# Channel-mix products on tiles of one batch in four pairs, in one fixed order with the attention before them

## The chip, the cores and the metric

The kernel runs on one NeuronCore of a Trainium2 chip. The metric is device time in microseconds of one execution. One execution was also recorded by the hardware profiler; times inside the kernel come from that record. TensorE is called PE, VectorE DVE, ScalarE ACT, and SyncE, which issues every DMA here, SP.

## What is computed

Attention with a sigmoid in place of the softmax, and behind it a channel mix on its output x (8 batches of 448 tokens, 768 features):

```python
scores = q @ k.T / sqrt(64) - log(448)          # 8 batches, 12 heads, 448 tokens, 64 features
x = sigmoid(scores) @ v                         # -> [8, 448, 768]
x_prev = x shifted by one token in each batch
xk = mu_k * x + (1 - mu_k) * x_prev
xr = mu_r * x + (1 - mu_r) * x_prev
k = maximum(xk @ w_k, 0)                        # 768 -> 1024
v = (k * k) @ w_v                               # 1024 -> 768
r = sigmoid(xr @ w_r)                           # 768 -> 768
out = r * v
```

The weights come as 64-bit floats and are converted on the chip; activations are 32-bit. 8 x 448 = 3584 tokens.

## The kernel before

**Attention** goes over 48 pairs of heads, `n` from 0 to 47, six pairs to a batch (`b, j = divmod(n, 6)`), two pairs to a pass of its loop. For each pair PE computes three score chunks of 128 keys (L341) into three score buffers `sc`, ACT turns each into `pf` by the sigmoid (L362), and PE multiplies `pf` with `v` into `av` (L369); the last 64 keys go in a tail (`score_tails` L350, `pt`, `weigh_tails` L377). `gather` copies `av` to `xx` (ACT, L387), makes the difference to the token before (`dx`, L388) and the two mixes `mr` and `mk` (L391) on DVE, and writes them to DRAM as `xr_d[j]` and `xk_d[j]`, columns of batch `b`. Beside this the conversion of `w_r` runs (`convert_seven`), with its results in seven buffers `slot`, and a first part of `w_k`.

**The products** come in three stages: R (`xr @ w_r`), K (`xk @ w_k`), V (`k*k @ w_v`). The weights are cut into four quarters, and two token tiles at a time are combined so that seven products do the work of eight (`ORDER`, products named `p` = 0 to 6 with weights in `slot` number `POS[p]`). One product of one pair of tiles is a *step*: for every row block `i` (3, 4, 3 in R, K, V) and contraction tile `t` (3, 3, 4) three matmuls (`multiply`, L556), high weight x high operand, high x low, low x high, since each 32-bit value is split into two parts. That is 27, 36 and 36 matmuls in a step of R, K and V. `right` makes a step's operands: `fetch` loads a tile into `ys`, `minus` (DVE, L464) forms sums of tiles, `operand` casts it on ACT (L472) and subtracts on DVE to get the low part (L473) into one of ten buffers `rr`. Four of the `ys` and `rr` are set aside from the start (`PRE`), the others (`ysb`, `rrb` in the trace) lie in memory that attention uses and can be filled only when attention is over. `evacuate` reads the sums from PSUM (`xb`, `yb`) on ACT and DVE; four matmuls (`prime`, L543) open the `yb` sums once.

A token tile is 512 tokens here, so a tile takes in parts of two batches. 3584 tokens are seven tiles: three pairs and a single one, for which four of the seven products suffice (`ODD`), two of which use the operands of the other two again. That is 3 x 7 + 4 = 25 steps in a stage.

**Order of the work.** `Plan` collects every operation with its engine, an estimated duration, a due time (`at`, in steps) and what it reads and writes. A list scheduler in `order` runs through it with estimated times and picks on each free engine the ready operation that is due first; `emit` issues them in that order. There are two plans, one for attention with the `w_r` conversion and one for the products, and each is issued inside a `tc.manual_schedule()` of its own, which keeps the order as issued. Between the two, outside of both, buffers are closed and opened. The framework below joins both lists, and an operation of the second whose buffers are free can come to stand among those of the first.

Of the kernel before, what the change touches and what calls it, by code (L numbers as in the profile page):

```python
# [8 lines left out]
F32 = mybir.dt.float32  # L9
# [13 lines left out]
class Plan:  # L23
# [8 lines left out]
    def op(self, engine, cost, prio, run, reads, writes, dma=None):  # L32
        i = len(self.ops)
        deps = set()
        for r in reads:
            if r in self.writer:
                deps.add(self.writer[r])
        for w in writes:
            if w in self.writer:
                deps.add(self.writer[w])  # L40
            deps.update(self.readers.get(w, ()))
        for r in reads:
            self.readers.setdefault(r, []).append(i)
        for w in writes:
            self.writer[w] = i
            self.readers[w] = []
        deps.discard(i)
        self.ops.append(Op(engine, cost, prio, run, deps, dma))
# [50 lines left out]
def attention_then_channel_mix(  # L99
# [16 lines left out]
    P = 128  # L116
    N, _, S = q.shape
# [2 lines left out]
    D = v.shape[-1]  # L120
    NP = DM // P
    B = N // NP
    T = 512
    NT = B * S // T
    NJ, NF = DM // P, DF // P
    NC = S // P
    KW = NC * P
# [5 lines left out]
    R_, K_, V_ = range(3)  # L133
# [10 lines left out]
    mur = const.tile([P, NJ], F32, name="mur")  # L144
    muk = const.tile([P, NJ], F32, name="muk")

    def scratch(name, n):
        return [dram.tile([P, B * S], F32, name=f"{name}{i}") for i in range(n)]

    xk_d, xr_d, r_d, k2_d = scratch("xk_d", NJ), scratch("xr_d", NJ), scratch("r_d", NJ), scratch("k2_d", NF)  # L150
# [10 lines left out]
    def ring(pool, name, bufs, shape, dtype):  # L161
        return [pool.tile(shape, dtype, name=f"{name}{i}") for i in range(bufs)]

    def gap(pool, name, size):
        pool.tile([P, size // 4], F32, name=name)
# [9 lines left out]
    gap(base, "gap0", 64)  # L175
    rr = ring(base, "rr", PRE, [P, 2, T], F32R)
    ys = ring(base, "ys", PRE, [P, T], F32)
    wraw = ring(base, "wraw", 2, [P, WP, 2], U32)
# [17 lines left out]
    mk = ring(apool, "mk", 2, [P, S], F32)  # L196
    mr = ring(apool, "mr", 2, [P, S], F32)
# [3 lines left out]
    plan = Plan()  # L201
# [7 lines left out]
    def act(n, sbuf=False, ptr=False):  # L209
        return 100 + 0.834 * n + 42 * sbuf + 93 * ptr  # L210

    def dve(n, fast=False, ptr=False):
        return 135 + n / (1.92 if fast else 0.96) + 61 * ptr
# [7 lines left out]
    def dma(dst, src, prio, reads, writes):  # L221
        ns = dst.shape[0] * math.prod(dst.shape[1:]) * 4 / 300
        op(SP, 500, prio, lambda: nc.sync.dma_start(dst, src), reads, writes, dma=ns)
# [74 lines left out]
        return put  # L298

    ORDER = (0, 1, 5, 4, 6, 2, 3)  # L300
    ODD = (0, 1, 6, 3)
    POS = {p: g for g, p in enumerate(ORDER)}

    def load(n, at):
# [78 lines left out]
    def gather(n, at):  # L383
        b, j = divmod(n, NP)
        x, d, X, G = xx[n % 2], dx[0], ("xx", n % 2), ("dx", 0)
        cols = slice(b * S, (b + 1) * S)
        op(ACT, act(S), at, lambda: nc.scalar.copy(x[:, 1:], av[n % 2][:, :S]), [("av", n % 2)], [X])  # L387
        op(DVE, dve(S), at, lambda: nc.vector.tensor_sub(d, x[:, 1:], x[:, :S]), [X], [G])  # L388
        for name, m, mu, to in (("mr", mr[n % 2], mur, xr_d), ("mk", mk[n % 2], muk, xk_d)):
            M = (name, n % 2)  # L390
            op(DVE, dve(S, ptr=True), at, lambda m=m, mu=mu: nc.vector.scalar_tensor_tensor(m, d, mu[:, j:j + 1], x[:, :S], ALU.mult, ALU.add), [X, G, (mu is muk, "mu")], [M])  # L391
            dma(to[j][:, cols], m, at, [M], [])

    load(0, -9)
    prepare(0, -9)
# [25 lines left out]
    for n in range(0, N, 2):  # L421
        at = n + 1
# [5 lines left out]
        at = n + 2  # L428
# [12 lines left out]
        nc.gpsimd.memset(t[:, 0:1], 0.0)  # L441

    nr = [0]
    used, kept = {}, {}

    def y_of(stage, role, t):
        i = role * KT[stage] + t
        return ys[i], ("y", i)

    SOURCE = {R_: xr_d, K_: xk_d, V_: k2_d}  # L450
    PAIRS = [(2 * s, 2 * s + 1) for s in range(NT // 2)] + [(NT - 1,)]

    def tokens(tile_):
        return slice(tile_ * T, (tile_ + 1) * T)

    def fetch(stage, s, role, t, at):
        y, Y = y_of(stage, role, t)
        ch, par = {0: (0, 0), 1: (1, 0), 3: (0, 1), 4: (1, 1)}[role]
        i, c = ch * KT[stage] + t, PAIRS[s][par]
        dma(y, SOURCE[stage][i][:, tokens(c)], at - 1, [("x", stage, i, c)], [Y])  # L460

    def minus(stage, dst, a, b, t, at):
        (d, D_), (x, X), (y, Y) = (y_of(stage, r, t) for r in (dst, a, b))
        op(DVE, dve(T), at, lambda: nc.vector.tensor_sub(d, x, y), [X, Y], [D_])  # L464

    def operand(stage, s, p, role, t, at):
# [4 lines left out]
        used.setdefault((stage, s, p), []).append((r, R))  # L471
        op(ACT, act(T, True), at, lambda: nc.scalar.copy(r[:, 0], y), [Y], [R])  # L472
        op(DVE, dve(T), at, lambda: nc.vector.tensor_sub(r[:, 1], y, r[:, 0]), [Y, R], [R + ("lo",)])  # L473


    def right(stage, s, p, at):
        if len(PAIRS[s]) == 1 and p in (6, 3):
            used[stage, s, p] = used[stage, s, {6: 0, 3: 1}[p]]
            return
        for t in range(KT[stage]):  # L480
            if p in (0, 1):
                fetch(stage, s, p, t, at)
                operand(stage, s, p, p, t, at)
            elif p == 5:
                fetch(stage, s, 3, t, at)
                minus(stage, 0, 3, 0, t, at)
                fetch(stage, s, 4, t, at)
                minus(stage, 2, 4, 0, t, at)
                operand(stage, s, p, 2, t, at)
            elif p == 4:  # L490
                operand(stage, s, p, 0, t, at)
            elif p == 6:
                minus(stage, 3, 3, 4, t, at)
                operand(stage, s, p, 3, t, at)
            elif p == 2:
                operand(stage, s, p, 4, t, at)
            elif p == 3:
                minus(stage, 2, 1, 2, t, at)
                operand(stage, s, p, 2, t, at)

    with tc.manual_schedule():
        plan.emit()
    att.close()
    psc.close()
    ps.close()

    pb = ctx.enter_context(tc.tile_pool(name="pb", bufs=1, space=PSUM))
    yb = ring(pb, "yb", 4, [P, T], F32)
    xb = ring(pb, "xb", 4, [P, T], F32)
    yb = yb[2:] + yb[:2]  # L510
    vp = ctx.enter_context(tc.tile_pool(name="vp", bufs=1, side="right"))
    ys += ring(vp, "ysb", 5 * NFH - PRE, [P, T], F32)
    u2 = ring(vp, "u2", 4, [P, T], F32)
# [4 lines left out]
    gap(vp, "gap4", 64)  # L518
    rr += ring(vp, "rrb", 6, [P, 2, T], F32R)

    plan = Plan()
    op = plan.op
    ncc, nrt, nw = [0], [0], [0]
# [37 lines left out]
    def finish(stage, s, half, par, i, src, R, c, at):  # L561
# [6 lines left out]
        rows = KT[R_] if stage != K_ else NFH  # L568
        m, tile_ = half * rows + i, PAIRS[s][par]
        cols = tokens(tile_)  # L570
# [18 lines left out]
    def evacuate(stage, s, p, i, at):  # L589
        X, Y, U, F = ("xb", i), ("yb", i), ("u2", i), ("p4", i)  # L590
        x, y = xb[i], yb[i]
        one = len(PAIRS[s]) == 1
        if p == 0:
            op(ACT, act(T), at, lambda: nc.scalar.copy(y, x), [X], [Y])  # L594
        elif p == 1:
            finish(stage, s, 0, 0, i, x, [X], None, at)
        elif p == 5:
            op(ACT, act(T), at, lambda: nc.scalar.copy(u2[i], y), [Y], [U])
        elif p == 4:
            op(ACT, act(T), at, lambda: nc.scalar.copy(p4[i], x), [X], [F])  # L600
        elif p == 6 and not one:
            op(DVE, dve(T), at, lambda: nc.vector.tensor_add(p4[i], y, p4[i]), [Y, F], [F])
            finish(stage, s, 1, 1, i, p4[i], [F], p4[i], at)
        elif p == 2:
            op(DVE, dve(T), at, lambda: nc.vector.tensor_add(u2[i], x, u2[i]), [X, U], [U])
            finish(stage, s, 0, 1, i, u2[i], [U], u2[i], at)
        elif p == 3:
            finish(stage, s, 1, 0, i, y, [Y], None, at)

    PREP, EVAC = -1.2, 0.3  # L610
    steps = [(stage, s, p) for stage in (R_, K_, V_) for s, pair in enumerate(PAIRS) for p in (ORDER if len(pair) == 2 else ODD)]
    first = {stage: next(i for i, x in enumerate(steps) if x[0] == stage) for stage in (R_, K_, V_)}
    last = {(stage, p): max(i for i, x in enumerate(steps) if x[0] == stage and x[2] == p) for stage in (R_, K_, V_) for p in range(7)}
    for stage, w, out7, pace in ((K_, w_k, wk_o, WK_PACE), (V_, w_v, wv_o, WV_PACE)):
        at = first[stage - 1]
# [1 line left out]
            convert_seven(w, t, KT[stage], CW[stage], pace, at, to_dram(out7, t, CW[stage]))  # L617
            at += 4 * pace
    for at, (stage, s, p) in enumerate(steps):
        right(stage, s, p, at + PREP)  # L620
        rows = NFH if stage == K_ else NJH
        if at == 0:
            for i in range(4):
                prime(i, 0.9)
        for i in range(rows):
            multiply(stage, s, p, i, at + i / rows)
            evacuate(stage, s, p, i, at + i / rows + EVAC)
        if stage < V_ and last[stage, p] == at:
            load_weight(stage + 1, p, max(at + 1.5, first[stage + 1] - 8 + POS[p]))
    with tc.manual_schedule():  # L630
        plan.emit()


_INS = ["q", "k", "v", "moe_mu_k", "moe_mu_r", "moe_w_k", "moe_w_v", "moe_w_r"]
# [37 lines left out]
```

## Time and profile before

| | us |
|---|---|
| median of 3 runs | 853.5 (852.8 to 855.59) |
| profiled execution | 852.84 |
| its span, first to last instruction | 851.1 |
| PE / DVE / ACT busy | 831.4 / 583.5 / 476.3 |
| DMA | 179.63 MB, mean 211 GB/s |
| mean granted PE clock | 0.989 |

A row of a group reads: line, engine, operation, output<-inputs, shape, count, then busy time in us, mean ns of one, and the idle time of the engine before them with what ended it. `PEld` is the load of weights into the array, which overlaps the matmul before it. Recorded matmuls overlap each other, so their pace is read from start to start. In the chain of waits a row is start, duration, and what the end of the kernel waited for in it. A row of a stretch gives from:to, length, then the busy time of each engine with the number of instructions (PE, PEld, DVE, ACT, POOL; with a line asked for, only the engines that run it), the granted PE clock, the DMA engines' busy share and GB/s. Line numbers are those of the kernel before; in the kernel after, most from 302 on are lower by one (L471 for L472), while L543 and L556 are the same in both.

### The profile page before, as it was taken

How to read it: one execution, taken by the hardware profiler on the slowest of the kernel's cores; microseconds unless marked ns; L12 is line 12 of the kernel's file. 1: busy time of each engine (PE TensorE's matmuls, PEld its weight loads, DVE VectorE, ACT ScalarE, POOL GpSimd, SP SyncE). 2: the span in 40 equal slices, each digit the busy share in tenths (PEclk: the TensorE clock that was granted, in tenths of full speed). 3: DMA queues.
4: the chain of work that ended last, by engine and by line, in shares of the span. 5: the costliest groups of instructions: out<-in, count | busy, mean ns of one | idle time of the engine just before them, and what ended most of it. 6: DMA issues, size and time to landing. Idle time of an engine off the chain costs nothing.

```text
span 851.1 us, 12546 instructions
## 1 busy us (share of the span) xinstructions
PE 831.4 (98%) x4297; PEld 593.5 (70%) x4297; DVE 583.5 (69%) x1040; ACT 476.3 (56%) x773; POOL 0.3 (0%) x6
## 2 busy tenths in 40 slices
PE   8998999998999899999999999999999999999998
PEld 4444544443444687888888888888888888888886
DVE  4878888886765698988887973725835486594621
ACT  6767877775774555556565564557565433333310
POOL 0000000000000000000000000000000000000000
PEclk9998999998999999999999999999999999999999
DMA  7886887796763796968789573336654476455432
GB/s 232 266 255 210 259 266 224 242 317 225 245 212 109 253 351 209 308 198 272 277 289 290 187 255 125 144 128 196 188 173 166 150 213 202 128 179 164 124 124 86
DMA packets 98128, 179.63 MB, mean 211 GB/s; under 512 B 11152, under 2 KB 45456, under 8 KB 98064
## 3 DMA queue, kind: packets, MB, share of 16 engines
q1 hardware_dynamic: 98064, 178.83, 64.4%
q8 instruction: 34, 0.56, 0.3%
q14 instruction: 30, 0.25, 0.1%
HBM read 109.06 MB, written 69.73 MB: 210 GB/s over the span
## 4 chain that ended last, share of the span: by engine, by line
PE 93%; DMA 3%; DVE 2%; issue 1%; ACT 1%; SPq 0%; DVEq 0%; ACTq 0%
PE xb L556 37%; PE yb L556 29%; PE av L369 12%; PE sc L341 11%; PE av L377 2%; PE sc L350 2%; DMA ys<-xr_d 1%; DMA xr_d<-mr 1%; DVE mr L391 0%; DVE mk L391 0%; DMA qn<-in_q 0%; DMA xk_d<-mk 0%; ACT xx L387 0%; DMA ysb<-xr_d 0%; ACT pt L362 0%
## 5 line engine op out<-in xcount | busy, mean ns | idle before, releaser
L556 PE MATMUL xb<-rrb,slot 128*128 128x512 f32 x816 | 198.4, 393 | 0.0
L556 PEld LDWEIGHTS xb<-rrb,slot 128*128 128x128 f32 x816 | 154.0, 189 | 33.8
L556 PE MATMUL yb<-rrb,slot 128*128 128x512 f32 x696 | 169.5, 391 | 0.0
L556 PEld LDWEIGHTS yb<-rrb,slot 128*128 128x128 f32 x696 | 130.6, 188 | 28.8
L362 ACT ACTIVATE pf<-sc 128x896 f32<-128x896 f32 x144 | 122.6, 933 | 42.0 <-PE sc L341 42.0
L556 PE MATMUL xb<-rr,slot 128*128 128x512 f32 x570 | 142.1, 394 | 3.2 <-ACT yb L594 3.1
L556 PEld LDWEIGHTS xb<-rr,slot 128*128 128x128 f32 x570 | 107.2, 188 | 28.2 <-ACT yb L594 3.5
L473 DVE TENSOR_TENSOR rrb<-ysb,rrb 128x512 fp32r<-128x512 f32 x106 | 70.6, 688 | 75.0 <-ACT rrb L472 74.9
L369 PE MATMUL av<-pf,vn 128*64 128x448 f32 x576 | 122.0, 560 | 0.0
L556 PE MATMUL yb<-rr,slot 128*128 128x512 f32 x393 | 100.0, 393 | 0.0
L556 PEld LDWEIGHTS yb<-rr,slot 128*128 128x128 f32 x393 | 73.8, 188 | 16.7
L472 ACT CAST rrb<-ysb 128x512 fp32r<-128x512 f32 x106 | 63.3, 619 | 34.7 <-PE xb L556 12.4
L369 PEld LDWEIGHTS av<-pf,vn 128*64 128x64 f32 x576 | 38.0, 139 | 61.9 <-issue 56.4
L341 PE MATMUL sc<-qh,kh 64*128 64x448 f32 x282 | 57.7, 405 | 7.6 <-ACT pt L362 5.6
L341 PEld LDWEIGHTS sc<-qh,kh 64*128 64x128 f32 x282 | 26.5, 185 | 45.7 <-ACT xx L387 15.5
L341 PE MATMUL sc<-ql,kh 64*128 64x448 f32 x282 | 52.0, 365 | 0.0
L341 PE MATMUL sc<-qh,kl 64*128 64x448 f32 x282 | 51.6, 363 | 0.0
L594 ACT COPY yb<-xb 128x512 f32<-128x512 f32 x40 | 22.8, 571 | 46.0 <-PE xb L556 46.0
L317 DVE TENSOR_TENSOR kl<-kn,kh 128x384 fp32r<-128x384 f32 x47 | 26.1, 555 | 29.0 <-ACT kh L216 28.9
L473 DVE TENSOR_TENSOR rr<-ysb,rr 128x512 fp32r<-128x512 f32 x46 | 30.6, 687 | 19.8 <-ACT rr L472 19.6
L388 DVE TENSOR_TENSOR dx<-xx 128x448 f32<-128x448 f32 x48 | 29.9, 622 | 20.8 <-ACT xx L387 20.3
L472 ACT CAST rr<-ysb 128x512 fp32r<-128x512 f32 x46 | 28.0, 621 | 24.9 <-DVE cc L586 11.2
(63 smaller groups left out, 872.9 us busy)
## 6 DMA issues: line engine op xcount, KB each, us to landing
kn<-in_k SPq DMA_DIRECT2D x48, 224.0 KB, 4.9
qn<-in_q SPq DMA_DIRECT2D x48, 224.0 KB, 5.1
vn<-in_v SPq DMA_DIRECT2D x48, 224.0 KB, 3.1
xr_d<-mr SPq DMA_DIRECT2D x48, 224.0 KB, 5.1
xk_d<-mk SPq DMA_DIRECT2D x48, 224.0 KB, 5.1
rt<-r_d SPq DMA_DIRECT2D x42, 256.0 KB, 3.0
ysb<-k_d SPq DMA_DIRECT2D x40, 256.0 KB, 2.8
k_d<-cc SPq DMA_DIRECT2D x32, 256.0 KB, 2.5
```

The lines of the kernel that those rows point to most:

```text
L317: op(DVE, dve(w), at, lambda src=src, hi=hi, lo=lo: nc.vector.tensor_sub(lo[i], src, hi[i]), R + [(a + "h", i)], [(a + "l", i)])
L341: nc.tensor.matmul(sc[u][:, h, :S], kk[half[h], c * P:(c + 1) * P], qq[half[h], :], start=e == 0, stop=e == len(pairs) - 1)
L350: nc.tensor.matmul(sc[u][half[h ^ (m % 2)], m % 2, :S], kn[m % RAW][half[h], KW:], qn[m % RAW][half[h], :], start=True, stop=True)
L362: op(ACT, 923, at, lambda: nc.scalar.activation(f, sc[u][:, :, :S], AF.Sigmoid, bias=NEG_LOG_S, scale=SCALE), R, [K])
L369: nc.tensor.matmul(av[n % 2][half[h], :S], vn[n % 5][:, h * NC + c, :], pf[i][:, h, :], start=c == 0, stop=False)
L377: nc.tensor.matmul(av[m % 2][half[r ^ (m % 2)], :S], vn[m % 5][half[r], 2 * NC, :], pt[n // 2 % PTB][half[r], m % 2, :], start=False, stop ...
L388: op(DVE, dve(S), at, lambda: nc.vector.tensor_sub(d, x[:, 1:], x[:, :S]), [X], [G])
L472: op(ACT, act(T, True), at, lambda: nc.scalar.copy(r[:, 0], y), [Y], [R])
L473: op(DVE, dve(T), at, lambda: nc.vector.tensor_sub(r[:, 1], y, r[:, 0]), [Y, R], [R + ("lo",)])
L556: nc.tensor.matmul(bank, a, b, start=p in (0, 4) and (t, e) == (0, 0), stop=(t, e) == (n - 1, 2), skip_group_check=True)
L594: op(ACT, act(T), at, lambda: nc.scalar.copy(y, x), [X], [Y])
```

## The change

A token tile becomes one batch, 448 tokens. There are eight, four pairs, and the single tile with its special cases goes. In every stage that makes 28 steps. `manual_schedule` is entered once and covers both plans and what lies between, so nothing of the second plan can come to stand within the first. `right(R_, 0, 0, ...)`, the operands of the very first step, is issued in the attention plan instead, due at the fourth-last head pair, with its fetches behind (`hold`) the last write of batch 6. DRAM writes of `gather` now name what they write.

```diff
-    T = 512
-    NT = B * S // T
+    T = S
+    NT = B
...
-    ODD = (0, 1, 6, 3)
...
-        for name, m, mu, to in (("mr", mr[n % 2], mur, xr_d), ("mk", mk[n % 2], muk, xk_d)):
+        for name, m, mu, to, stage in (("mr", mr[n % 2], mur, xr_d, R_), ("mk", mk[n % 2], muk, xk_d, K_)):
...
-            dma(to[j][:, cols], m, at, [M], [])
+            dma(to[j][:, cols], m, at, [M], [("x", stage, j, b)])
...
-    used, kept = {}, {}
+    used, hold = {}, []
...
-    PAIRS = [(2 * s, 2 * s + 1) for s in range(NT // 2)] + [(NT - 1,)]
+    PAIRS = [(2 * s, 2 * s + 1) for s in range(NT // 2)]
...
-        dma(y, SOURCE[stage][i][:, tokens(c)], at - 1, [("x", stage, i, c)], [Y])
+        dma(y, SOURCE[stage][i][:, tokens(c)], at - 1, [("x", stage, i, c)] + hold, [Y])
...
-    with tc.manual_schedule():
-        plan.emit()
+    hold.append(("x", R_, NJ - 1, B - 2))
+    right(R_, 0, 0, N - 4)
+    ctx.enter_context(tc.manual_schedule())
+    plan.emit()
...
+    hold.clear()
     plan = Plan()
...
-        right(stage, s, p, at + PREP)
+        if (stage, s, p) not in used:
+            right(stage, s, p, at + PREP)
...
-    with tc.manual_schedule():
-        plan.emit()
+    plan.emit()
```

The PSUM tiles `xb` and `yb` keep 512 columns of which 448 are used. How the instructions stand is not seen in this. Three places follow; numbers behind the names are buffers.

ACT, before, near the start of attention (about head pair 9): the casts of the first step's operands `rr` from the fetched `ys`, among sigmoids (`pf`, `pt`) and weight casts (`slot`).

```order
L362 ACTIVATE pf_170<-sc_184 128x896
L472 CAST rr_125<-ys_129 128x512
L362 ACTIVATE pf_171<-sc_185 128x896
L291 CAST slot_118<-wbits_140 128x384
L291 CAST slot_122<-wbits_135 128x384
L216 CAST kh_161<-kn_142 128x384
L216 CAST qh_156<-qn_152 128x448
L472 CAST rr_126<-ys_130 128x512
```

The same casts in the kernel after, in the last two passes of attention:

```order
L361 ACTIVATE pt_175<-sc_185 128x896
L361 ACTIVATE pf_166<-sc_186 128x896
L471 CAST rr_125<-ys_129 128x448
L361 ACTIVATE pf_167<-sc_184 128x896
L471 CAST rr_126<-ys_130 128x448
L471 CAST rr_127<-ys_131 128x448
L361 ACTIVATE pf_168<-sc_185 128x896
```

Three casts moved from the first quarter of attention to its end; a fourth, of `rr_128` for the second step, stood at some 70% of it before and stands behind all of attention now.

SP, where attention ends, as a piece of the difference: the last writes of `gather`, then fetches for the second and third steps.

```order
 L223 DMA xr_d_76<-mr_183 128x448
 L223 DMA xk_d_70<-mk_181 128x448
-L223 DMA ysb_2494<-xr_d_75 128x512
-L223 DMA ysb_2495<-xr_d_76 128x512
-L223 DMA ysb_2499<-xr_d_71 128x512
...
+L223 DMA wraw_133<-in_moe_w_k 128x1024
+L223 DMA ys_132<-xr_d_74 128x448
+L223 DMA ysb_2502<-xr_d_75 128x448
+L223 DMA ysb_2503<-xr_d_76 128x448
+L223 DMA ysb_2507<-xr_d_71 128x448
```

A fetch of raw weights (`wraw`) and that of the fourth operand (`ys_132`), which stood within attention before, now stand ahead of the first fetches into attention's memory.

PE at the same place, before: the last attention matmuls, the four priming ones, the first step (weights `slot_117`) and the second (`slot_118`).

```order
L377 MATMUL av_188<-pt_176,vn_148 64x448 x2
L543 MATMUL yb_2485<-rr_125,slot_117 128x512
L543 MATMUL yb_2486<-rr_125,slot_117 128x512
L543 MATMUL yb_2483<-rr_125,slot_117 128x512
L543 MATMUL yb_2484<-rr_125,slot_117 128x512
L556 MATMUL xb_2487<-rr_125,slot_117 128x512 x3
L556 MATMUL xb_2487<-rr_126,slot_117 128x512 x3
```

After:

```order
L376 MATMUL av_188<-pt_176,vn_148 64x448 x2
L556 MATMUL xb_2495<-rr_125,slot_117 128x448 x3
...
L556 MATMUL xb_2497<-rr_127,slot_117 128x448 x3
L543 MATMUL yb_2493<-rr_125,slot_117 128x448
L543 MATMUL yb_2494<-rr_125,slot_117 128x448
L543 MATMUL yb_2491<-rr_125,slot_117 128x448
L543 MATMUL yb_2492<-rr_125,slot_117 128x448
L556 MATMUL xb_2495<-rr_128,slot_118 128x448 x3
```

The first step now goes directly behind attention, and the priming matmuls stand between it and the second.

More of the change, by code (lines that the diff above doesn't have):

```diff
@@ L476, in right @@
     def right(stage, s, p, at):
-        if len(PAIRS[s]) == 1 and p in (6, 3):
-            used[stage, s, p] = used[stage, s, {6: 0, 3: 1}[p]]
-            return
         for t in range(KT[stage]):
@@ L507, in attention_then_channel_mix @@
     pb = ctx.enter_context(tc.tile_pool(name="pb", bufs=1, space=PSUM))
-    yb = ring(pb, "yb", 4, [P, T], F32)
-    xb = ring(pb, "xb", 4, [P, T], F32)
-    yb = yb[2:] + yb[:2]
+    yb = ring(pb, "yb", 4, [P, 512], F32)
+    xb = ring(pb, "xb", 4, [P, 512], F32)
+    yb = [b[:, :T] for b in yb[2:] + yb[:2]]
+    xb = [b[:, :T] for b in xb]
     vp = ctx.enter_context(tc.tile_pool(name="vp", bufs=1, side="right"))
@@ L591, in evacuate @@
         x, y = xb[i], yb[i]
-        one = len(PAIRS[s]) == 1
         if p == 0:
@@ L600, in evacuate @@
             op(ACT, act(T), at, lambda: nc.scalar.copy(p4[i], x), [X], [F])
-        elif p == 6 and not one:
+        elif p == 6:
             op(DVE, dve(T), at, lambda: nc.vector.tensor_add(p4[i], y, p4[i]), [Y, F], [F])
@@ L610, in attention_then_channel_mix @@
     PREP, EVAC = -1.2, 0.3
-    steps = [(stage, s, p) for stage in (R_, K_, V_) for s, pair in enumerate(PAIRS) for p in (ORDER if len(pair) == 2 else ODD)]
+    steps = [(stage, s, p) for stage in (R_, K_, V_) for s in range(len(PAIRS)) for p in ORDER]
     first = {stage: next(i for i, x in enumerate(steps) if x[0] == stage) for stage in (R_, K_, V_)}
```

## The prediction, made before the changed kernel was run

> **What bounds the kernel now.** I read the page first (shares, chain), then the chain in order of time and the product line (L556) by stretches, then the places where TensorE (PE) waits, then VectorE (DVE) beside the first products.
>
> ```profile
> span 851.1 us, 12546 instructions
> PE 831.4 (98%) x4297; PEld 593.5 (70%) x4297; DVE 583.5 (69%) x1040; ACT 476.3 (56%) x773; POOL 0.3 (0%) x6
> PE 93%; DMA 3%; DVE 2%; issue 1%; ACT 1%; SPq 0%; DVEq 0%; ACTq 0%
> ```
>
> PE sets the end: the chain of work that ended last runs through it for 93% of the span. What is not PE in it, 7%, sits at few places, shown below. So two things count: how long PE needs per matmul times how many there are, and those places.
>
> The product matmuls by stretches (first step, then all others), and four steps from the chain:
>
> ```profile
> 274.00:283.30 9.30, 6.33 (x27) 4.87 (x26) 1.00 0.59 185
> 283.30:847.30 564.00, 563.77 (x2448) 460.66 (x2448) 1.00 0.61 200
> ...
> 283.38 8.09 PE xb L556 x27
> ...
> 297.61 6.25 PE xb L556 x27
> ...
> 525.36 8.36 PE yb L556 x36
> ...
> 657.66 8.18 PE yb L556 x36
> ...
> 814.37 16.49 PE xb L556 x72
> ```
>
> The second stretch is one unbroken run: 2448 matmuls of 512 columns from 283.4 to 847.3, 563.9 us. Its steps give the pitch, start to start: 6.25/27 = 231 ns, 8.36/36 = 232, 8.18/36 = 227, 16.49/72 = 229. The step at 283.38 took 8.09 instead of about 6.2, 1.9 us more, after a wait. Another 0.2 us is a short wait at 335.4 that I come to. So 561.8/2448 = 229.5 ns is the pitch, with 227 as its floor.
>
> **The change, part by part.**
>
> *Count and pitch of the product matmuls.* A step is rows x contraction tiles x 3 matmuls: 27, 36 and 36 in the three stages, 99 for one step of each. Before there are 3 pairs of 7 steps and a single tile of 4, 25 steps: 25 x 99 = 2475, the sum of the x27 and x2448 above. After there are 4 pairs of 7, 28 steps: 2772, each with 448 columns instead of 512. 12% more matmuls, 12.5% fewer columns. Columns times matmuls fall by 2%, which is 11 us only if the pitch goes with the columns. The trace has no 128x128 product with 448 columns; nearest are the attention scores, which have the same operand type and 448 columns, as two matmuls side by side on half the rows each. Consecutive pairs:
>
> ```profile
> 9.25 0.36 PE L341 MATMUL sc<-qh,kl 64*128 64x448 f32 x2
> 9.45 0.37 PE L341 MATMUL sc<-ql,kh 64*128 64x448 f32 x2
> 9.65 0.36 PE L341 MATMUL sc<-qh,kh 64*128 64x448 f32 x2
> 9.86 0.36 PE L341 MATMUL sc<-qh,kl 64*128 64x448 f32 x2
> 10.05 0.36 PE L341 MATMUL sc<-ql,kh 64*128 64x448 f32 x2
> 10.26 0.36 PE L341 MATMUL sc<-qh,kh 64*128 64x448 f32 x2
> ```
>
> Five pitches in 1.01 us: 202 ns, single ones 190 to 210 (rounded to 10). Proportion from the products says 229.5 x 448/512 = 200.8. I take 201. Low end: the floor in proportion, 227 x 0.875 = 198.5. High end 205: the score pitch plus the 3 ns by which slow product steps exceed the mean.
>
> What could stop the pitch from shrinking is the weight load before every matmul:
>
> ```profile
> L556 PEld LDWEIGHTS xb<-rrb,slot 128*128 128x128 f32 x816 | 154.0, 189 | 33.8
> L341 PEld LDWEIGHTS sc<-qh,kh 64*128 64x128 f32 x282 | 26.5, 185 | 45.7 <-ACT xx L387 15.5
> ```
>
> The load takes 189 ns and its unit idles 33.8/816 = 41 ns per matmul, so at 201 it would still have 12 ns. The score loads, 185 ns, do run at a pitch of 202. It is tight, but fits.
>
> After the first step, 2745 x 201 = 551.7 us. I keep the slow first matmuls and the short wait, 2.1 us: 553.8 against 563.9, **-10.1 us** (198.5 ns: -17; 205 ns: +0.9).
>
> The Trainium skill ("TensorE: Matmul & The Clock Gate", Back-to-back issue gap) gives columns/2.4 + 2.5 ns, 215.8 at 512. This trace does not agree, at 229.5. By the rule's slope alone, 26.7 ns for 64 columns, the pitch would be 202.8 and the term -5.1 us instead of -10.1.
>
> *The waits in attention.* Attention repeats every 10.54 us (75.09 to 85.63 below, the same place of the loop). From the chain, and two casts of the timeline:
>
> ```profile
> 46.99 2.41 PE av L369 x12
> 53.15 6.51 DMA xr_d<-mr
> 59.72 3.17 DMA ys<-xr_d
> 75.09 2.41 PE av L369 x12
> 85.63 2.41 PE av L369 x12
> ...
> 169.83 2.40 PE av L369 x12
> 192.63 4.84 DMA ys<-xr_d
> 207.42 2.41 PE av L369 x12
> ...
> 62.91 0.62 ACT L472 CAST rr<-ys 128x512 fp32r<-128x512 f32 x1 [4.75 <-DMA ys<-xr_d]
> 197.50 0.62 ACT L472 CAST rr<-ys 128x512 fp32r<-128x512 f32 x1 [2.70 <-DMA ys<-xr_d]
> ```
>
> Two periods after 46.99 is 68.07, but PE got there at 75.09: 7.0 us lost. Three periods after 169.83 is 201.45, but it was 207.42: 6.0 us. Both times ScalarE (ACT), in order, stood at a cast of a first-product operand whose fetch (ys<-xr_d) had not landed, with the sigmoids queued behind it that free the score banks. The first fetch had itself waited for xr_d<-mr to land, since 512 tokens reach into the second batch. After the change these three fetches stand after batch 6's last write and their casts most of a loop pass later, on data of batch 0 that landed long ago; the fourth operand's comes after attention. Both waits go: **-13.0 us**. The three casts now stand among the sigmoids of the last head pairs: 3 x 0.62 = 1.9 us of ACT, in a stretch without the weight casts (slot<-wbits) that it carries earlier. One loop pass there, before the change:
>
> ```profile
> 253.00:264.00 11.00, 11.00 (x84) 5.20 (x76) 5.39 (x10) 7.21 (x11) 0.00 (x0) 1.00 0.32 106
> ```
>
> ACT (fourth pair of columns) is busy 7.2 of 11 us, so most of the 1.9 finds room. Between 0 and 1.9 I take **+0.5**, nearer the covered end.
>
> *The junction.* PE's last attention matmul and first product steps, with what released them:
>
> ```profile
> 270.86 0.98 PE L377 MATMUL av<-pt,vn 64*64 64x448 f32 x8
> 272.94 1.20 PE L543 MATMUL yb<-rr,slot 128*128 128x512 f32 x4 [1.10 <-ACT xx L387]
> 276.50 2.58 DMA xk_d<-mk
> 279.66 2.58 DMA ysb<-xr_d
> 283.38 1.05 PE L556 MATMUL xb<-rr,slot 128*128 128x512 f32 x2 [3.05 <-ACT yb L594]
> ```
>
> The second step cannot start before its operands: last gather, write to DRAM (276.50, landed 279.08), then the fetch into memory that attention has just freed (landed 282.24), then cast and subtraction. That is 283.38 - 271.84 = 11.5 us after attention, whatever PE does in between. The change lets the first step run ahead of the four priming matmuls, so PE loses the 1.1 us wait, and the step is 27 x 28 ns = 0.8 us shorter: both only lengthen the wait before the second step, from 3 us to some 5. **0 us.** A 512 KB weight fetch now stands ahead of the fourth operand's fetch in SP's queue, and four conversion instructions ahead of its subtraction on DVE: up to +2. The first three matmuls need only that operand and can go early: down to -1.5.
>
> *VectorE beside the first products.* Cover for the operand work is DVE's idle time in the first stage:
>
> ```profile
> 283.00:322.00 39.00, 38.62 (x161) 31.42 (x162) 36.10 (x63) 22.69 (x42) 0.00 (x0) 0.96 0.90 313
> 322.00:366.00 44.00, 43.85 (x192) 35.56 (x191) 38.85 (x67) 24.78 (x45) 0.00 (x0) 1.00 0.74 253
> ...
> 434.00:641.00 207.00, 207.00 (x903) 169.34 (x902) 127.36 (x214) 122.78 (x212) 0.00 (x0) 1.00 0.59 194
> ...
> L473 DVE TENSOR_TENSOR rrb<-ysb,rrb 128x512 fp32r<-128x512 f32 x106 | 70.6, 688 | 75.0 <-ACT rrb L472 74.9
> L317 DVE TENSOR_TENSOR ql<-qn,qh 128x448 fp32r<-128x448 f32 x46 | 28.5, 619 | 0.1
> ...
> PEld xb L556 <- DVE rr L473: 0.6, 1, 0.6
> ```
>
> DVE (third pair of columns) is busy 36.1 of 39 and 38.85 of 44 us there, because w_k's conversion shares it; PE waited for it once, 0.6 us. In those 83 us PE does 13 steps; after, each is 27 x 28.5 ns = 0.77 us shorter, so 73 us remain. About 75 operand and evacuation instructions shrink from 688 to 619 ns, -5.2 us; the conversion does not shrink, and 1.6 us of it moves in from attention: 75.0 - 5.2 + 1.6 = 71.4 of 73. Some of that runs ahead for later steps, so it can just hold, with little slack for ACT's late casts. Bounds: 0, or all of it needed plus the 8 us of idle that remain today, 79.4 - 73 = 6.4. I take **+2**, nearer the covered end because only one wait shows at 90% load. The second stage has room (DVE 127 of 207 us): its five more operand sets (28 instead of 23, as the single tile used two of its four twice), 3 tiles each, are 15 subtractions of 0.62 us, 9 us, and hide behind PE. The DMA bytes of a stage stay the same. The tail after the last matmul, some 4 us, stays.
>
> **Sum.** The profiled execution took 852.84 us: the span and 1.74 around it. 852.84 - 10.1 - 13.0 + 0.5 + 0 + 2 = 832.2. The median of the runs, 853.5, lies 0.66 above it: 833 us.
>
> **Rivals.**
>
> A. VectorE becomes the bound of the first stage, and stalls grow beyond the 6.4 us, since the order is fixed and each late subtraction also holds the evacuations behind it: 837 to 846. For it: 71.4 of 73 us. Against: slack in front of PE grew to several us by 366 in the run before, with one wait of 0.6.
>
> B. The waits in attention do not vanish but move: casts behind a late fetch near the last heads. One wait like the second costs 6 us: 839; both, 846. Against: the batch-0 data is old and fetch and cast stand most of a 10.54 us pass apart.
>
> C. Slower than before: the pitch does not go with the columns, because load and hand-over (189 + 41 ns) are a chain of their own. At 229.5 ns, 2745 matmuls take 630 us, +76 on the forecast: 909. It decides from 208 to 209 ns upward, where 2745 x pitch eats the 13.0 - 2.5 us gained elsewhere (563.9 + 10.5 - 2.1 = 572.3; /2745 = 208.5). Against it, the scores' 202 ns with loads of 185.
>
> D. The extra over a streaming time belongs to 512 columns, so 448 goes at 189 to 190 ns, the load's own time and the shortest score pitch by its rounding: 2745 x 189.5 = 520, 801 us. That is also where the skill's formula in full would put it (189.2 ns). The five score pitches, 202 on average, speak against.
>
> E. No change that shows: the gains of attention eaten by A and C in part. "Shows" means over 0.3%, 2.6 us.
>
> **Chances.** Forecast 0.75, A 0.09, B 0.06, C 0.05, D 0.03, E 0.02. Faster by over 0.3%: forecast, A, B and D, 0.93; within 0.3%: 0.02; slower: 0.05. Range: 833 - 7 (floor pitch) - 1.5 for the low end, 825; for the high end the 205 ns pitch (+11), or A or both waits of B, 845. C, D and E stay outside, 0.10.
>
> **What would show it.** Right: product steps of 5.4 us (27) and 7.2 us (36) in the chain; no ys<-xr_d in the chain during attention and 10.54 us periods throughout; attention's last matmul near 259; the second step still 11.5 us behind it; from there about 554 us to the last matmul. Wrong: steps of 27 above 5.6 us (C); PE waiting for rr or rrb of line 473's counterpart in the first stage for more than 6 us together (A); a fetch in the chain near the last heads (B).

## The result and the profile after

The changed kernel takes 835.1 us, the median of 4 runs (834.55 to 835.75), beside 853.81 us for the kernel before on the same chip (4 runs, 852.8 to 855.59). The ratio is 0.9779, its 95% interval 0.9761 to 0.9797: 18.7 us, 2.2%, faster. The forecast was 833 us in a range of 825 to 845. Two executions at a far slower pace, 1668.35 us of the order alone and 1178.37 us of the kernel before, are in none of the medians and ratios that follow.

The profiled execution took 835.32 us with a span of 833.5, beside 852.84 and 851.1. The two spans differ by 17.6 us, and that difference is taken apart here. Each row is cut at a matmul that both traces have:

| stretch of TensorE's work | before, us | after, us | difference | forecast |
|---|---|---|---|---|
| span's start to the first weighted product (`av`) | 10.95 | 11.81 | +0.86 | 0 |
| first to last `av` group of attention | 255.25 | 242.20 | -13.05 | -13.0 + 0.5 |
| from there to the second step's first matmul | 17.18 | 18.02 | +0.84 | 0 |
| second step's first to the last matmul's start | 563.60 | 557.56 | -6.04 | -10.1 + 2 |
| from there to the span's end | 4.09 | 3.87 | -0.22 | 0 |

The page of the changed kernel begins like that of before: span, busy time of each engine, and the shares of the chain.

```profile
span 833.5 us, 13485 instructions
PE 819.3 (98%) x4594; PEld 647.9 (78%) x4594; DVE 618.8 (74%) x1160; ACT 492.0 (59%) x857; POOL 0.3 (0%) x6
PE 97%; DMA 1%; issue 1%; DVE 1%; ACT 0%; SPq 0%; ACTq 0%; DVEq 0%
```

TensorE (PE) holds 97% of the chain instead of 93%, and DMA 1% instead of 3%. There are 297 more matmuls (4594 against 4297), and yet PE is busy 12 us less.

The product line by the same two stretches as before (length, PE busy, weight load busy, granted clock, DMA share, GB/s):

```profile
260.70:271.90 11.20, 5.67 (x27) 4.98 (x27) 1.00 0.69 221
272.00:829.90 557.90, 557.19 (x2745) 516.28 (x2745) 1.00 0.63 203
```

And steps of the chain in order of time (start, duration, engine, output, line, count):

```profile
53.98 2.41 PE av L368 x12
64.48 2.41 PE av L368 x12
...
180.28 2.41 PE av L368 x12
190.83 2.41 PE av L368 x12
201.37 2.41 PE av L368 x12
...
272.03 7.21 PE xb L556 x27
285.83 5.46 PE xb L556 x27
...
422.84 14.59 PE xb L556 x72
437.43 7.21 PE yb L556 x36
444.64 7.30 PE xb L556 x36
```

The later steps give 5.46/27 = 202.2, 14.59/72 = 202.6, 7.21/36 = 200.3 and 7.30/36 = 202.8 ns. Over all records from the second step on, with the waits and the slow first matmuls left out, the mean pitch is 202.07 ns; before it is 229.45. Attention's groups stand 10.5 us apart at the two places where 7.0 and 6.0 us were lost before, and so do all others of the loop.

The junction between attention and products, from the timeline (start, duration, engine, work, idle time before it and what ended that):

```profile
258.67 0.98 PE L376 MATMUL av<-pt,vn 64*64 64x448 f32 x8
260.75 5.67 PE L556 MATMUL xb<-rr,slot 128*128 128x448 f32 x27 [1.10 <-ACT xx L386]
265.43 0.42 SPq L223 DMA_DIRECT2D wraw<-in_moe_w_k  x1
265.90 0.45 SPq L223 DMA_DIRECT2D ys<-xr_d  x1
266.26 0.97 PE L543 MATMUL yb<-rr,slot 128*128 128x448 f32 x4
270.98 0.56 ACT L471 CAST rr<-ys 128x448 fp32r<-128x448 f32 x1 [10.28 <-DMA ys<-xr_d]
272.03 1.49 PE L556 MATMUL xb<-rr,slot 128*128 128x448 f32 x3 [4.80 <-ACT yb L593]
```

The chain a little later, at the third step:

```profile
279.70 1.03 ACT rrb L471 x2
280.75 0.64 DVE rrb L472
281.44 2.74 PE yb L556 x12
```

The second step begins 12.4 us after attention's last matmul (259.65); in the kernel before it was 11.5. The wait is named after ACT's copy to `yb`, which empties the PSUM bank that the second step writes next. In ACT's order this copy stands behind the cast of the fourth operand, and that cast had stood 10.28 us for its fetch. The third step then waits about 1.1 us for an operand that ScalarE (ACT) and VectorE (DVE) make.

The windows of the stretch that the forecast feared, with the engines in the order PE, weight load, DVE, ACT, POOL:

```profile
272.00:305.00 33.00, 32.44 (x149) 29.15 (x150) 32.48 (x62) 19.42 (x39) 0.00 (x0) 0.95 0.94 316
305.00:345.00 40.00, 39.85 (x197) 36.59 (x197) 36.35 (x68) 23.38 (x47) 0.00 (x0) 1.00 0.79 270
```

DVE is busy 98% and 91% of the time there, and PE still loses only 0.15 us of the 40 after 305.

### The profile page after: what moved, and what is told of

The parts are those of the page before. It is cut to its first block, busy times and chain, and to the rows that moved or that the text cites. A ratio compares the mean times of both kernels' runs of the same rounds, so it can differ in the third digit from the quotient of the medians.

```text
span 833.5 us, 13485 instructions
## 1 busy us (share of the span) xinstructions
PE 819.3 (98%) x4594; PEld 647.9 (78%) x4594; DVE 618.8 (74%) x1160; ACT 492.0 (59%) x857; POOL 0.3 (0%) x6
## 4 chain that ended last, share of the span: by engine, by line
PE 97%; DMA 1%; issue 1%; DVE 1%; ACT 0%; SPq 0%; ACTq 0%; DVEq 0%
PE xb L556 38%; PE yb L556 29%; PE av L368 13%; PE sc L340 12%; PE av L376 3%; PE sc L349 2%; DMA ys<-xr_d 1%; DMA qn<-in_q 0%; SPq L223 0%; ACT rrb L471 0%; DVE mr L390 0%; DVE dx L387 0%; DVE mk L390 0%; DVE rrb L472 0%; DVE cc L586 0%
## 5 line engine op out<-in xcount | busy, mean ns | idle before, releaser
L556 PE MATMUL xb<-rrb,slot 128*128 128x448 f32 x993 | 214.2, 366 | 0.0
L556 PEld LDWEIGHTS xb<-rrb,slot 128*128 128x128 f32 x993 | 187.3, 189 | 15.1 <-DVE rrb L472 0.2
L556 PE MATMUL yb<-rrb,slot 128*128 128x448 f32 x675 | 148.7, 366 | 0.5 <-ACT rrb L471 0.3
L556 PE MATMUL xb<-rr,slot 128*128 128x448 f32 x591 | 130.8, 365 | 6.1 <-ACT yb L593 4.8
L556 PE MATMUL yb<-rr,slot 128*128 128x448 f32 x513 | 113.4, 363 | 0.0
L472 DVE TENSOR_TENSOR rrb<-ysb,rrb 128x448 fp32r<-128x448 f32 x112 | 67.1, 620 | 48.1 <-ACT rrb L471 47.8
L471 ACT CAST rrb<-ysb 128x448 fp32r<-128x448 f32 x112 | 60.9, 565 | 19.0 <-PE yb L556 12.9
L472 DVE TENSOR_TENSOR rr<-ysb,rr 128x448 fp32r<-128x448 f32 x80 | 47.3, 620 | 30.1 <-ACT rr L471 30.1
L471 ACT CAST rr<-ysb 128x448 fp32r<-128x448 f32 x80 | 43.9, 567 | 27.7 <-PE yb L556 17.7
L471 ACT CAST rrb<-ys 128x448 fp32r<-128x448 f32 x56 | 30.7, 563 | 25.1 <-PE xb L556 17.9
```

What stands on the lines that cost most here:

```text
L556: nc.tensor.matmul(bank, a, b, start=p in (0, 4) and (t, e) == (0, 0), stop=(t, e) == (n - 1, 2), skip_group_check=True)
```

## The experiments

**The order without the tiles.** The kernel before, with 512 columns and its three pairs and a single tile, under one schedule as after and with the first operands made during attention:

```diff
-    with tc.manual_schedule():
-        plan.emit()
+    hold.append(("x", R_, NJ - 1, B - 2))
+    right(R_, 0, 0, N - 4)
+    ctx.enter_context(tc.manual_schedule())
+    plan.emit()
...
+    hold.clear()
...
-        right(stage, s, p, at + PREP)
+        if (stage, s, p) not in used:
+            right(stage, s, p, at + PREP)
```

> The kernel before with the fixed order alone: one manual order over both plans and the first step's operands made during attention; tiles stay at 512 tokens, 25 steps. Theory (two separate gains, 13.0 us from the waits in attention and the rest from the pitch of the products): the two waits at 60 and 191 us are gone, attention's first to last weighted product takes 242.2 us instead of 255.3, the product pitch stays at 229.5 ns, and the time is about 853.8 - 13 + 1 for the longer junction = 841 to 842 us. Rival (the waits go because a 448-token tile no longer reaches into the second batch, the order is beside the point): the waits stay or move, and the time is 848 us or more.

Measured: 843.64 us (median of three), ratio 0.9881 (0.9865 to 0.9898), 10.2 us faster: some 2 us short of the theory's gain, and far from the rival's 848. Where the rest of the 13 us went is seen in a later run of the same kernel.

**The tiles without the order.** The kernel after with its two plans scheduled separately and no operand made in attention by name:

```diff
-    hold.append(("x", R_, NJ - 1, B - 2))
-    right(R_, 0, 0, N - 4)
-    ctx.enter_context(tc.manual_schedule())
-    plan.emit()
+    with tc.manual_schedule():
+        plan.emit()
...
-    plan.emit()
+    with tc.manual_schedule():
+        plan.emit()
```

> The changed kernel with the order of before: two separate manual orders, operands of the first step made by the second plan, tiles of 448 tokens, 28 steps. Theory (two separate gains): product pitch 202 ns as in the changed kernel, casts of the first step's operands stand early in attention again; at least one of them waits for its fetch, attention loses 4 to 13 us, and the time is 840 to 848 us. Rival (the 448-token tile alone removes the waits, since batch 0 is complete sooner): attention takes 242 us without waits and the time is 835 to 836 us.

Measured: 843.48 us, ratio 0.9891 (0.9871 to 0.991), 10.3 us faster. In its profiled execution (841.51 us) the pitch is that of the changed kernel, 202.08 ns. Attention takes 249.74 us: three of its periods are 13.98, 11.84 and 13.38 us instead of 10.54. Its chain shows the fetches back in attention:

```profile
24.05 5.46 DMA xr_d<-mr
29.58 3.00 DMA ys<-xr_d
...
190.50 4.42 DMA ys<-xr_d
```

The waits (total us, times, longest):

```profile
ACT rr L471 <- DMA ys<-xr_d: 8.6, 4, 3.6
```

And two of the casts in the timeline:

```profile
31.63 0.56 ACT L471 CAST rr<-ys 128x448 fp32r<-128x448 f32 x1 [2.40 <-DMA ys<-xr_d]
194.94 0.57 ACT L471 CAST rr<-ys 128x448 fp32r<-128x448 f32 x1 [2.28 <-DMA ys<-xr_d]
```

ACT still stood at these casts, 8.6 us in 4 waits. So a tile that ends with the batch lets the first fetch start earlier (29.58 us instead of 59.72) and shortens what attention loses from 13.05 to 7.5 us, but only the place of the casts in ACT's order removes it. The pitch belongs to the tiles alone. The one schedule and the operands made in the plan of attention came together in these runs; what either does without the other was not run.

**What the pitch is made of.** In the changed kernel all but the first matmul of each block of rows (a block has 9 matmuls in the first two stages, 12 in the third) get fewer columns: 416, 384 and 320 in the three stages. The other columns of the products are left out.

```diff
-    nc.tensor.matmul(bank, a, b, start=..., stop=..., skip_group_check=True)
+    z = T if (t, e) == (0, 0) else (416, 384, 320)[stage]
+    nc.tensor.matmul(bank[:, :z], a, b[:, :z], start=..., stop=..., skip_group_check=True)
```

> The changed kernel with narrower moving operands: apart from the first matmul of each row block, every product matmul takes only the first 416 (stage R), 384 (stage K) or 320 (stage V) of 448 columns, so those products lack columns. Theory 1 (at 448 columns the weight load, 188 ns plus its hand-over of some 14 ns, already sets the pitch of 202): the pitch stays at 198 to 202 ns in all three stages and the time stays within 4 us of the changed kernel's 835. Theory 2 (the pitch goes with the columns, 229.5/512 = 0.448 ns for each): 186, 172 and 143 ns, less 12, 27 and 52 us with the first matmuls kept wide, about 750 us. Theory 3 (columns/2.4 plus a constant 13 ns, without a floor): 187, 173 and 147 ns, nearly the same as theory 2.

Measured: 749.6 us in one run. The product line by a stretch of each stage (the matmul and load busy times, clock, DMA share, GB/s):

```profile
273.00:405.00 132.00, 130.52 (x680) 127.59 (x679) 0.99 0.84 284
420.00:580.00 160.00, 160.00 (x907) 158.67 (x907) 1.00 0.67 219
600.00:745.00 145.00, 144.26 (x954) 142.74 (x953) 1.00 0.70 223
```

160.0/907 = 176 ns and 145/954 = 152 ns still hold the one full matmul of each block. Of the narrowed ones alone the pitch is 188.3 ns at 416 columns, 173.8 at 384 and 146.5 at 320. One line through these and the two widths of the kernels, 8.2 + 0.432 x columns, gives 187.9, 174.1, 146.4, 201.7 and 229.4 ns beside 188.3, 173.8, 146.5, 202.0 and 229.5. There is no floor at the load's 188 ns. The last stage's load records explain that (busy us, mean ns):

```profile
L557 PEld LDWEIGHTS xb<-rrb,slot 128*128 128x128 f32 x353 | 53.8, 188 | 0.5
```

353 loads of 188 ns make 66 us of records in 53.8 us of busy time: the records overlap, so a record is longer than the time that its load holds up the next. The rival that the load bounds the pitch falls.

**The junction.** In the changed kernel the conversion of `w_k` in the first product steps starts two steps later:

```diff
-        at = first[stage - 1]
+        at = first[stage - 1] + 2 * (stage == K_)
```

> The changed kernel with the rest of w_k's conversion due two steps later, so that its first 512 KB fetch stands behind the second and third steps' operand fetches instead of ahead of them, and its DVE instructions behind the first subtractions. Theory (the 0.84 us by which the junction grew, 11.54 to 12.38, is this fetch ahead of ys in the queue, 5.05 us to land): junction back to 11.5 us or a little under, the wait of 1.07 us in the third step gone too, 1 to 2 us less than the changed kernel, 833 to 834 us. Rival (the junction is set by the gather's last write and the memory that becomes free after it): no change, 835 us.

Measured: 833.94 us, ratio 0.9774 (0.9752 to 0.9796). The changed kernel beside it on the same chip took 833.89 us, so nothing changed that can be measured. The trace does what was meant: the third step's wait and the short one later are gone (555.80 us from the second step to the last matmul, against 557.48 beside it), and the junction is 11.28. But the profiled execution, 831.95 us, was the shortest of four by 1.8 us. So the sharing of DVE with the conversion costs at most 1 to 2 us, and the runs do not resolve it.

**Two steps early.** Six operands instead of four made during attention, so that the second step needs nothing from behind it:

```diff
-    WP, PFB, PTB, LEAD, RAW = 512, 9, 2, 2, 4
+    WP, PFB, PTB, LEAD, RAW = 512, 8, 2, 2, 4
...
-    PRE = 4
+    PRE = 6
...
+    right(R_, 0, 1, N - 3)
...
-    rr += ring(vp, "rrb", 6, [P, 2, T], F32R)
+    rr += ring(vp, "rrb", 10 - PRE, [P, 2, T], F32R)
```

> The changed kernel with the operands of the second step made during attention as well: two more ys and rr buffers are set aside (PRE 6), and one of nine sigmoid buffers pf is given up for the room. Theory (the 4.8 us wait and the eight matmuls at half pace behind it, 1.4 us, are the price of the second step's operands alone): PE runs first step, priming and second step in one piece, the slow matmuls vanish, a wait of 0 to 2 us remains before the third step; 4 to 6 us less than the changed kernel, 829 to 831 us. Rival (the wait moves on to the third step, which needs fetches into the same freed memory): the wait before the third step is 3 us or more with slow matmuls behind it, and 1 to 3 us are gained, 832 to 834 us. If eight pf buffers are too few, attention gets longer than 242.2 us, first to last weighted product, and the gain shrinks by that.

Measured: 832.86 us (830.95 to 836.51, 5 runs), ratio 0.9776 (0.9746 to 0.9806), 1.0 us below the changed kernel beside it, less than the spread. Attention is 242.13 us, so one buffer fewer costs nothing. The second step starts 7.64 us after attention, as meant. But the timeline of PE:

```profile
267.91 5.68 PE L557 MATMUL xb<-rr,slot 128*128 128x448 f32 x27
274.36 0.44 PE L557 MATMUL yb<-rrb,slot 128*128 128x448 f32 x1 [0.77 <-issue]
275.39 0.68 PE L557 MATMUL yb<-rrb,slot 128*128 128x448 f32 x2 [0.59 <-DVE rrb L472]
276.52 0.74 PE L557 MATMUL yb<-rrb,slot 128*128 128x448 f32 x1 [0.46 <-ACT rrb L471]
278.15 2.21 PE L557 MATMUL yb<-rrb,slot 128*128 128x448 f32 x4 [0.89 <-DVE rrb L472]
```

The third step now waits in pieces for the first operands made in attention's freed memory. With the slow matmuls behind these waits the products lose 6.7 us over the pitch, against 3.3 beside it. The wait moved one step on, as the rival had it. The chain to the last of these rows runs through a fetch of raw weights (`wraw`, 6.10 us), whose conversion stands ahead of the subtractions in DVE's order.

**Both of these.** The last kernel with the conversion two steps later.

> Both of the two before: second step's operands made during attention, and w_k's conversion two steps later. Theory: the third step's fetches no longer stand behind 512 KB of weights, its wait goes, 1 us less than with the second step's operands alone, 828 to 830 us. Rival: DVE, with the conversion pushed together towards the middle of the first stage, makes PE wait there, and nothing or less is gained.

Measured: 834.54 us, ratio 0.9785 (0.976 to 0.9811): no gain. The junction grew to 13.5 us:

```profile
270.40 0.57 ACT L471 CAST rrb<-ys 128x448 fp32r<-128x448 f32 x1 [10.28 <-DMA ysb<-xr_d]
272.00 1.39 ACT L594 COPY yb<-xb 128x448 f32<-128x448 f32 x3
272.58 2.98 PE L557 MATMUL xb<-rr,slot 128*128 128x448 f32 x7 [5.92 <-ACT yb L594]
```

The second step had its operands, but not its PSUM banks. The copy that empties them (`yb<-xb`) stood in ACT's order behind casts for the third and fourth steps, the first of which waited 10.28 us for its fetch. So neither the theory nor the rival had it. The second plan's clock starts at zero, as if DMA were free at that moment, and so it can place casts ahead of their fetches; the last variant below changes this alone.

**The changed kernel again, beside these.**

> The changed kernel once more beside the three others on the same chip, as their measure: 834.5 to 835.8 us.

Measured: 833.89 us, ratio 0.9781 (0.976 to 0.9803). Its junction is 11.54 us, not 12.38, with the weight fetch at the same place in the queue. So that place is not what made the 0.84 us of the first profile, although the theory of the conversion experiment had it so.

**The order alone, looked at.** The kernel of the first experiment once more.

> The kernel before with the fixed order alone once more, for a trace at full PE pace. It took 843.7 us where 841 to 842 were expected. Theory (the waits in attention are gone, the rest is the junction): attention 242.1 to 242.2 us without long periods, the product pitch 229.5 ns, and the missing 2 us lie between attention's end and the third step: a junction of 12 us or more, or more matmuls at half pace. Rival (a wait in attention is left): a period of the attention loop over 10.6 us.

Measured: 842.55 us in one run. Attention is 242.14 us with no long period, the pitch 229.47 ns. From the chain:

```profile
263.36 2.70 DMA xk_d<-mk
266.65 3.70 DMA ysb<-xr_d
271.55 8.95 PE xb L559 x27
281.01 1.14 ACT rrb L472 x2
282.92 4.83 PE yb L559 x20
```

The junction is 12.85 us (+1.3 against before), and the stretch from the second step on has 3.6 us of waits and slow matmuls in it, against 2.1. So the order alone takes the whole 13 us from attention and gives back some 2.8 us at the first two places where operands are short.

**A planner that knows of the wait.** The kernel of "both" with the second plan's DMA clock (its unit is the plan's ns) set later:

```diff
-    plan = Plan()
+    plan = Plan(dma_from=8000)
```

> Second step's operands made during attention, w_k's conversion two steps later, and the second plan told that no transfer of its own lands in its first 8 us (Plan(dma_from=8000)). Theory (the second step waited 5.9 us in e6 for a copy that stood on ACT behind casts whose fetches had not landed; the plan put them there since it counts time from its own start and lets fetches land at once): the copies yb<-xb now stand ahead of those casts, PE runs first step, priming and second step in one piece (second step 7 to 8 us after attention), the third starts 13 to 15 us after attention's end with few slow matmuls behind it; 4 us less than the changed kernel in the same call, 829 to 831 us. Rival (the time is given back at the third and fourth steps, whose operands come late whatever the order): third step more than 15 us after attention's end, and the time within 2 us of the changed kernel's.

Measured: 832.92 us (829.3 to 835.53, 6 runs), ratio 0.9749 (0.9724 to 0.9774). The copy now goes first and the second step runs 7.63 us after attention; what is left stands right behind it:

```profile
265.94 1.39 ACT L594 COPY yb<-xb 128x448 f32<-128x448 f32 x3 [6.02 <-PE yb L544]
266.51 5.68 PE L557 MATMUL xb<-rr,slot 128*128 128x448 f32 x27
274.21 0.67 PE L557 MATMUL xb<-rrb,slot 128*128 128x448 f32 x2 [1.82 <-DVE rrb L472]
276.40 1.72 PE L557 MATMUL xb<-rr,slot 128*128 128x448 f32 x5 [1.33 <-DVE rr L472]
```

These rows are most of one row block of the fourth step (nine matmuls into `xb`). The new order has this block ahead of the third step, and PE waits in it for operands; the third step's 27 matmuls into `yb` start at 277.92, 19 us after attention's end (258.88). So the copy was placed as the theory said, and the rest of the time was given back behind it, as the rival said.

**The changed kernel beside that one.**

> The changed kernel beside the one before, as its measure: 833.5 to 835.8 us.

Measured: 834.92 us, ratio 0.9783 (0.977 to 0.9796), junction 11.54 us. The last variant is 2.0 us below it by the medians. Its interval (0.9724 to 0.9774) overlaps this one only between 0.977 and 0.9774, so it is probably the faster, by some 0.2%, and not more than that can be said. The two traces show little of it: from attention's end to the last matmul they take 569.1 and 569.5 us.

## Why the prediction was right

The mechanism was as forecast: a shorter pitch, and no waits in attention. The total, 835.1 against 833, is 2.1 us off; terms erred in both directions, so a part of that nearness is luck. The terms, by their steps:

- *Pitch, -10.1 us: right in kind, too large.* Measured is -7.0 us. The pitch was taken as 201 ns by proportion to the columns and came out at 202.07, where the score rows of the prediction had stood (202); 2745 x 1.07 = 2.9 us. The width experiment shows what proportion leaves out: each matmul has about 8.2 ns that do not go with its columns. Proportion cuts these by an eighth too, and 2772 x 8.2/8 = 2.8 us is that error. The Trainium skill ("TensorE: Matmul & The Clock Gate", Back-to-back issue gap) puts a fixed part beside one that goes with the columns, as these runs do. By its slope alone the pitch was 202.8 ns, 0.7 off where mine was 1.1 off. Its formula in full, which it gives for isolated matmuls, has 135.8 ns at 320 columns and 189.2 at 448; the runs have 146.5 and 202.1, so its sizes do not hold here.
- *The weight load "is tight, but fits": the conclusion holds, its reason does not.* At 320 columns loads recorded at 188 ns follow each other every 146.5 ns. The idle time of 41 ns beside the load was no margin that could be used up, and the pitch was not near a floor.
- *Attention, -13.0 us: right, with one part of the loss unnamed.* Measured is -13.05. The tile alone leaves 7.5 us of the loss, the order alone none, so the place of the casts decides, as the prediction said. What the prediction did not name is that the waits are only 7.6 us of the 13.0 lost before; the clock behind them makes most of the rest (rows below). It read the loss from the periods, which hold both, so the sum came out. The three casts were put at +0.5 us and cost nothing that shows: attention is 242.12 to 242.20 us in five traces that contain them, with every period at 10.5 us.
- *Junction, 0 us: right.* It is +0.84 us in the first profile and 11.54 us, as before, in two more of the same kernel. One step in it was wrong: PE was said to lose the 1.1 us wait after attention, but the first step stands in the same wait for the same ACT copies (`[1.10 <-ACT xx L386]`). It made no difference, as the wait before the second step, 4.80 us against "some 5", takes up any such gain.
- *DVE in the first stage, +2 us: right in kind, too large.* Waits and slow matmuls in the products are 3.03 us against 2.11, so +0.9, of which the third step's wait is about 1.1. The load of DVE was put at 71.4 of 73 us; it is 32.48 + 36.35 = 68.8 of the 73 from 272 to 345.
- *What the sum did not have.* The first 12 score matmuls took 4.85 us instead of 4.02, which makes the +0.86 at the start: after, each of the twelve is recorded with 951 ns or more; before, the last four with some 537. In other profiles of these kernels the first `av` group stands between 10.9 and 12.5 us, so this differs from one execution to the next.

The kernel before, where attention waited (TensorE's timeline, then the clock behind the first wait; the granted clock is the third number from the end):

```profile
64.40 0.47 PE L341 MATMUL sc<-qh,kh 64*128 64x448 f32 x2 [1.98 <-ACT pf L362]
67.86 0.74 PE L341 MATMUL sc<-qh,kh 64*128 64x448 f32 x2 [2.58 <-ACT pt L362]
199.42 0.74 PE L341 MATMUL sc<-qh,kh 64*128 64x448 f32 x2 [3.07 <-ACT pt L362]
...
65.20:71.90 6.70, 4.12 (x16) 1.83 (x16) 6.70 (x15) 5.46 (x9) 0.00 (x0) 0.50 0.68 220
```

PE stood 4.56 us of the 7.0 lost at the first place and 3.07 of the 6.0 at the second. Behind both waits its granted clock is 0.50 (from 198.3 to 205.0 too), and the twelve weighted products there took 3.72 and 4.50 us instead of 2.41.

Of the rivals, DVE as the bound (A) did not come, nor waits that move to the last heads (B: all periods are equal), nor a pitch held by the load (C), nor one at 189.5 ns (D: 202.07). In sum the profiled execution is 3.1 us above its forecast (835.32 against 832.2). The pitch makes 3.1 of it, and the start and this execution's junction 1.7. DVE and the casts, put too high, take back 1.7, and the tail 0.2. The rest is rounding and 0.1 us more around the span.

## What to carry to other kernels

Cost a matmul as a fixed part and a part for each column, both from records of two widths; proportion through zero flatters narrow tiles, since it shrinks the fixed part along with the columns. A cast that waits for a fetch on an in-order engine costs what is queued behind it, and the clock behind the wait can cost nearly as much again (3.07 us of waiting, 6.0 lost), so move the cast in the order rather than hurry the fetch, and give the planner of the following stage the time at which transfers can really land. Here, making operands for one more step ahead moved the wait to the first step that still needed the freed memory, and the gain was at most 2 us.

## What the runs showed of the hardware that was not expected

The weight-load records are no occupancy: loads of 188 ns mean in the records followed at 146.5 ns, and they overlap.

Behind some waits PE goes on at half pace, and the profile's granted clock shows it. Behind the wait before the second step these are 7 to 15 matmuls, at a pitch of 373 ns with 448 columns and 427 with 512. In the changed kernel, 7 of them followed the wait of 4.80 us:

```profile
271.80:275.20 3.40, 3.17 (x9) 2.79 (x10) 3.40 (x7) 2.09 (x6) 0.00 (x0) 0.50 1.02 385
```

That is 7 x 171 ns = 1.2 us more than the wait itself shows. The Trainium skill ("TensorE: Matmul & The Clock Gate", Back-to-back issue gap) gives columns/1.2 for the slow state, 373.3 and 426.7 ns, and these records agree. In the two kernels where the second step follows the priming matmuls without a wait, no slow matmul stands there, and none stands behind the 1.10 us wait after attention in the two kernels compared here. It came behind shorter waits close together, though: 0.46 to 0.89 us with the second step's operands made early (granted clock 0.50 from 276.5 to 283.2), 1.82 and 1.33 us in the last variant (from 277.1 to 280.4). So how long a wait has to be is open. Two of the six runs of the last variant had a mean granted clock of 1.00 and took 829.3 us; the others had 0.995 to 0.998 and took 832.0 to 835.5. So the slow stretch may come or not with the execution; those two were not traced.
